# The next to last row stored as the last one is: x added on VectorE, plain stores by SyncE and ScalarE

## The chip, the cores and the metric

The kernel runs on 1 core of one Trainium2 chip. The metric is the time of one execution on the device, in microseconds (us). A profiled execution has a span, from its first to its last instruction, which is a little shorter than the time.

## The reference

```python
def reference(A_x, A_w_r, A_w_i, B_x, B_w1, B_b1, B_w2, B_b2):
    ...
    def _A_ref(x, w_r, w_i):                  # spectral filter over tokens and channels
        X = jnp.fft.rfft2(x) * (w_r + 1j * w_i)
        return jnp.fft.irfft2(X, s=(S, D))
    def _B_ref(x, w1, b1, w2, b2):            # MLP over the token axis
        h = _layernorm(x, axis=-1)
        u = _gelu(jnp.einsum("bsd,sf->bdf", h, w1) + b1)
        y = jnp.einsum("bdf,fs->bds", u, w2) + b2
        return y.transpose(0, 2, 1)
    x = A_x                                   # (1, 2048, 512) float32
    xn = _layernorm(x, axis=-1)
    s = _A_ref(xn, A_w_r, A_w_i)
    g = _silu(_B_ref(xn, B_w1, B_b1, B_w2, B_b2))
    return x + s * g
```

Tokens S = 2048, channels D = 512, hidden size F = 1792. Only the last operation, `x + s * g`, and how its result reaches the output are touched here.

## The kernel before

The 2048 tokens are laid out as 128 partitions by 16 rows (`NJ = 16`), so a row `j` is a tile of 128 tokens by 512 channels, 256 KB in float32. The kernel first normalizes and transforms the rows and forms the hidden layer (TensorE, with split high and low parts of the float32 operands), then filters the spectrum, and in its last part makes the outputs.

The last part is a loop over `p` from 0 to 7 (`NP = 8`). Pass `p` makes the gate `g` of two rows, `j0 = p` and `j1 = p + 8`, out of seven matrix products of half blocks taken in the order 1, 2, 5, 6, 3, 7, 4 (a Strassen scheme; `products`, `copied`, `summed`, `gate`). The weight blocks for it (`a11`, `a12`, `a21`, `s1`, `s4`) are loaded ahead from `w2`. The block `s1` of pass `p` lies in one of two tiles with the tag `s1`: in the pool `w2p` for even `p`, in the pool `fp` for odd `p`.

The spectral part `s` of a pair of rows is transformed back on TensorE into banks 0 and 1 of the accumulation memory (`spectral`), one pass behind the gates. `finish(g, j, cols)` then multiplies it by the gate on VectorE, in two instructions, because the channels are stored folded (`mirrored`), and stores the row in two halves of 64 partitions (`halved`).

Adding x is done in two ways. Early in the kernel, x is copied to the output for rows 0 to 14 (`out[q, :NJ - 1]`, L498), and `finish` for these rows adds `s * g` to it with an accumulating store issued by GpSimd (`accum_op`). For row 15 alone x is loaded into `xr` (SyncE, in the last pass at `k == 2`, into the tile `s1` of the pool `fp`, free once the pass's block `s1` is read), VectorE adds it, and the sum is stored plainly.

In passes 1 to 7 `finish` runs for the rows of the pass before. In the last pass it runs besides for that pass's own rows, 7 and 15: at `k == 5`, behind the sixth of the seven products, for row 7 whole and for row 15's right half (`right_`); after the loop, for row 15's left half, whose gate needs the seventh product. Those results go into the tile `rows` (`last_rows`). Stores of row 15 are issued by SyncE for partitions 0 to 63; for partitions 64 to 127 by SyncE for the right half and by ScalarE for the left.

In this last part each engine's instructions keep the order in which the program gives them. At the end of the program (shown in the profile as L1099) SyncE waits for all transfers to land, every engine runs a drain, and the engines meet.

Of the kernel before, what the change touches and what calls it, by code (L numbers as in the profile page):

```python
# [9 lines left out]
F32 = mybir.dt.float32  # L10
# [6 lines left out]
P = 128  # L17
S, D, F = 2048, 512, 1792
NJ = 16
NF = F // P  # L20
EPS = 1e-5
NH = NF // 2
# [120 lines left out]
def spectral_mixer_kernel(tc, x, w1, b1, w2, b2, wk, we, wx, c_f, c_ft, c_d, c_i, c_g, c_h, c_t, out):  # L143
    nc = tc.nc
    V, A, G, T, SY = nc.vector, nc.scalar, nc.gpsimd, nc.tensor, nc.sync

    def pool(stack, side, name, bufs):
        return stack.enter_context(tc.tile_pool(name=name, bufs=bufs, side=side, reuse_waits="tile"))


    def mirrored(t, turned):
        v = t.rearrange("p (h q c) -> p h q c", q=2, c=P)
        return v[:, :, 0], v[:, :, 1, ::-1] if turned else v[:, :, 1]
# [9 lines left out]
    with tc.tile_pool(name="ps", bufs=1, space=PSUM) as psp, ExitStack() as left, ExitStack() as right:  # L163
# [320 lines left out]
        for j in range(NJ):  # L484
# [49 lines left out]
            if more:  # L534
                low(w[1][1], raws[j + 1, 1], w[1][0])
                if FIRST <= j < FIRST + NE:
                    i = j - FIRST
# [210 lines left out]
        for n in range(8):  # L748
            a, b, c, d, e, f = PACE[n]
# [11 lines left out]
        w2p = pool(right, "right", "w2", 3)  # L761
        NP, HD = NJ // 2, D // 2
# [38 lines left out]
        def sums_of_blocks():  # L801
            added_up("a12", "s1")
            added_up("a11", "a12")
# [60 lines left out]
        def banks(p):  # L864
            return ps[:, 2 + p % 2, :HD], ps[:, 4, :HD], ps[:, 5, :HD]

        def products(p, n):

            wf = ready.pop(0)
            bx, by, bz = banks(p)  # L870
            o = {1: bx, 6: bx, 7: bx, 4: bx, 2: by, 5: bz, 3: bz}[n]

            for a, (wi, ui) in enumerate(((0, 0), (0, 1), (1, 0))):
                for m, i in enumerate(FORMS):
                    T.matmul(o, wf[:, wi, i], form_parts(n, i)[ui], start=m + a == 0 and n in (1, 2, 5),
                             stop=m == NH - 1 and a == 2, skip_group_check=n in (6, 3, 7, 4))

        def copied(name, src, where):
            t = where.tile([P, HD], F32, name=name, tag=name.split("_")[0], bufs=1)
            step(A.activation(t, src, AF.Copy))  # L880
            return t
# [16 lines left out]
        V, A, SY, G = (Kept(e, keep) for e in (nc.vector, nc.scalar, nc.sync, nc.gpsimd))  # L898
        fp = pool(left, "left", "fin", 1)
        halved = (slice(0, 64), slice(0, None, 2)), (slice(64, P), slice(1, None, 2))  # L900
# [5 lines left out]
        def new_gates(p):  # L906
            return [fp.tile([P, D], F32, name=f"g{j}", tag="g", bufs=4) for j in (p, p + NP)]
# [6 lines left out]
        def gathered(p):  # L914


            yt = fp.tile([P, 2, 4, 2, 64], F32, name=f"yt{p}", tag="yt")
            yts[p] = yt
            for i, j in enumerate((p, p + NP)):
                for h in range(2):  # L920
                    to = yt[:, i, :, h ^ i].rearrange("p b (s c) -> p b s c", c=2)
                    yield V.tensor_copy(to, ey[:, :, h::2, j]) if i else A.activation(to, ey[:, :, h::2, j], AF.Copy)
# [29 lines left out]
        def unfolded(p):  # L952

            es, y = new_sums(p) if p else first_sums
            e0, e1 = (es[:, :, k].rearrange("p i b c -> p i (b c)") for k in range(2))
            if "E" in PARTS[p]:
                first, odd = ps[:, 6, :256].rearrange("p (i s c) -> p i s c", s=2, c=64), ps[:, 6:8, 256:]
                other = y.rearrange("p i h q c -> p (i h q c)")[:, :257]
                A.activation(other, ps[:, 7, :257], AF.Copy)
                other = other[:, :256].rearrange("p (i s c) -> p i s c", s=2, c=64)  # L960

                V.tensor_add(es[:, :, 1, :, :64], first, other)
                V.tensor_sub(es[:, :, 1, 0, :63:-1], first[:, :, 0], other[:, :, 0])
                V.tensor_sub(es[:, :, 1, 1, :63:-1], other[:, :, 1], first[:, :, 1])
                V.tensor_add(e0, e1, odd)
                V.tensor_sub(e1, e1, odd)
            else:
                pe = ps[:, 6:8].rearrange("p i (h k) -> p i h k", h=2)
                A.activation(e1, pe[:, :, 1], AF.Copy)
                V.tensor_add(e0, pe[:, :, 0], e1)  # L970
                V.tensor_sub(e1, pe[:, :, 0], e1)
            yield
            u, v = es[:, :, :, 0], es[:, :, :, 1]
            V.tensor_add(y[:, :, :, 0], u, v)
            yield
            V.tensor_sub(y[:, :, ::-1, 1], u, v)
            ys[p] = y.rearrange("p i h q c -> p i (h q c)")
            yield
# [9 lines left out]
        def gate(g, j, cols, src, scale):  # L988
            A.activation(g[:, cols], src, AF.Silu, bias=b2t[:, j:j + 1], scale=scale)

        def summed(name, a, b):
            t = fp.tile([P, HD], F32, name=name, tag="c", bufs=2)
            V.tensor_add(t, a, b)
            return t

        def finish(g, j, cols):
            r = last_rows[:, j // NP] if last_rows is not None else fp.tile([P, D], F32, name=f"r{j}", tag="r", bufs=2)
            for to, a, b in zip(mirrored(r[:, cols], True), mirrored(ps[:, j // NP, cols], False), mirrored(g[:, cols], False)):
                V.tensor_mul(to, a, b)
            if j + 1 == NJ:  # L1000
                V.tensor_add(r[:, cols], r[:, cols], xr[:, cols])
            for queue, (rows, tokens) in zip((SY, SY if cols is right_ else A), halved):
                if j + 1 < NJ:
                    G.dma_start(out[tokens, j, cols], r[rows, cols], accum_op=ALU.add)
                else:
                    queue.dma_start(out[tokens, j, cols], r[rows, cols])

        yts, ys, pieces = {}, {}, iter(())
        last_rows = None

        for p in range(NP):
            j0, j1 = p, p + NP
            more = p + 1 < NP
            if p:
                gates[p] = new_gates(p)
            g0, g1 = gates[p]
            bx, by, bz = banks(p)
            slot, plan = SLOTS[min(p, 1) + (not more)]
            gathering = gathered(p)
            for k, n in enumerate(ORDER):  # L1020
                started = not p and k < 2
                if not started:
                    products(p, n)
                if n == 1 and p:
                    p1 = copied(f"p1_{p}", bx, w2p)
                elif n == 5:
                    p5 = copied(f"p5_{p}", bz, fp)
                elif n == 6:
                    v2 = copied(f"v2_{p}", bx, fp)
                elif n == 7:  # L1030
                    c22 = summed(f"c22_{p}", bx, p5)
                if not started:
                    ready.extend(w for w in [next(wforms, None)] if w is not None)
                if n == 2:
                    c11 = summed(f"c11_{p}", by, p1)
                elif n == 6:
                    gate(g0, j0, left_, c11, 1.0)
                elif n == 3:
                    gate(g0, j0, right_, summed(f"c12_{p}", bz, v2), 1.0)
                elif n == 7:  # L1040
                    gate(g1, j1, right_, c22, -1.0)
                elif n == 4:
                    gate(g1, j1, left_, bx, -1.0)
                if k == slot:
                    for part in PARTS[p]:
                        {"S": spectral, "E": even_channels, "O": odd_channels, "F": channels}[part](p - (part == "S"))
                    yts.pop(p)
                    pieces = unfolded(p)
                    if p:
                        for g, j in zip(gates.pop(p - 1), (j0 - 1, j1 - 1)):  # L1050
                            finish(g, j, whole)
                for what in plan.get(k, ""):
                    next(gathering if what == "g" else pieces)
                if more and n == 7:
                    sums_of_blocks()
                if not more and k == 2:
                    xr = fp.tile([P, NH * P], F32, name="xr", tag="s1", bufs=1)[:, :D]
                    for rows, tokens in halved:
                        SY.dma_start(xr[rows], x[tokens, NJ - 1])
                if not more and k == 5:  # L1060
                    spectral(p)
                    last_rows = fp.tile([P, 2, D], F32, name="rows", tag="yt")
                    finish(g0, j0, whole)
                    finish(g1, j1, right_)
# [38 lines left out]
```

## Time and profile before

| | us |
|---|---|
| time, median of 3 runs | 372.07 (371.99 to 372.15) |
| profiled execution, span | 370.2 |
| profiled execution, time beside its span | none given |
| TensorE busy (share of the span) | 360.1 (97%) |
| VectorE busy | 304.9 (82%) |
| ScalarE busy | 210.9 (57%) |
| GpSimd busy | 86.8 (23%) |
| last matrix product ends | 362.2 |
| last computation ends (VectorE, row 15's left half) | 363.7 |

The profiler calls TensorE's products PE and its weight loads PEld, VectorE DVE, ScalarE ACT, GpSimd POOL and SyncE SP; a q behind the name is the engine's queue of instructions (waits, drains, issues of transfers), which is not counted as busy. Nearly all instructions stand under L140, the helper `Kept`, which records every operation, so they are told apart by their tiles: `rows`, `r`, `xr`, `out_dram`. A row of a group or a timeline gives the output tile, an arrow and the input tiles, then shapes and count.

### The profile page before, as it was taken

To read this page: it belongs to the slowest core of one execution; us is meant where nothing else is said; L and a number is where in the kernel's file an instruction comes from. 1 tells how busy PE (TensorE), PEld (TensorE's weight loads), DVE (VectorE), ACT (ScalarE), POOL (GpSimd) and SP (SyncE) were. 2 spreads that over 40 slices of the span, in tenths; PEclk is the share of its full clock that TensorE was granted. 3 is DMA by queue.
4 is the path that set the end of the run, shared out by engine and by line. 5 is a ranking of instruction groups with operands and counts; after the bars stand their busy time and mean duration, and the time that the engine had idled before them with its cause. 6 is when DMAs were issued, how large, how long until landed. Compare 5 with 4: busy or idle time off the path is not lost.

```text
span 370.2 us, 8760 instructions
## 1 busy us (share of the span) xinstructions
PE 360.1 (97%) x3442; PEld 308.5 (83%) x3442; DVE 304.9 (82%) x585; ACT 210.9 (57%) x381; POOL 86.8 (23%) x128
## 2 busy tenths in 40 slices
PE   7999999999999999999999999999999999999991
PEld 4778888778777778777888999999898989898981
DVE  4799999974899988989994978696878788787971
ACT  3797887748634445655336686545564646464520
POOL 3133333332222012221020001040505050413131
PEclk9999999999999999999999999999999999999997
DMA  7976997505694698695585487797989899897443
GB/s 192 248 189 169 241 289 225 227 2 150 177 276 166 188 272 229 179 241 184 173 278 106 113 248 139 229 138 215 178 206 190 194 202 184 211 188 161 74 58 57
DMA packets 33289, 68.40 MB, mean 185 GB/s; under 512 B 4736, under 2 KB 19504, under 8 KB 33120
## 3 DMA queue, kind: packets, MB, share of 16 engines
q1 hardware_dynamic: 24192, 42.04, 41.1%
q0 software_dynamic: 8656, 25.27, 32.3%
q10 hardware_dynamic: 400, 0.52, 0.5%
q8 instruction: 27, 0.44, 0.5%
q14 instruction: 14, 0.11, 0.1%
HBM read 59.43 MB, written 8.13 MB: 183 GB/s over the span
## 4 chain that ended last, share of the span: by engine, by line
PE 94%; DMA 2%; DVE 1%; issue 0%; POOL 0%; ACT 0%; POOLq 0%
PE ps L140 94%; DMA x<-in_x_dram 2%; DVE stm L220 0%; DVE rows L140 0%; POOL w1r L431 0%; ACT g L140 0%; DVE w1l L448 0%; DVE mvm L230 0%; POOL qm L436 0%; DVE v2m L225 0%; DVE v2m L224 0%; POOLq L436 0%
## 5 line engine op out<-in xcount | busy, mean ns | idle before, releaser
L140 PE MATMUL ps<-h,w1h 128*128 128x512 f32 x400 | 116.5, 398 | 0.7 <-DVE nbm L239 0.7
L140 PEld LDWEIGHTS ps<-h,w1h 128*128 128x128 f32 x400 | 72.8, 188 | 20.6 <-issue 4.9
L140 PE MATMUL ps<-h,w1l 128*128 128x512 f32 x200 | 68.1, 392 | 0.3 <-DVE w1l L448 0.2
L140 DVE TENSOR_TENSOR w2f<-a,w2f 128x896 fp32r<-128x896 f32 x36 | 39.3, 1091 | 22.1 <-ACT w2f L140 22.1
L140 PEld LDWEIGHTS ps<-h,w1l 128*128 128x128 f32 x200 | 37.2, 188 | 9.8 <-DVE w1l L448 1.9
L140 ACT ACTIVATE w2f<-a 128x896 fp32r<-128x896 f32 x36 | 36.9, 1024 | 12.6 <-PE ps L140 8.0
L140 PE MATMUL ps<-fb,w2f 128*128 128x256 f32 x336 | 41.9, 279 | 0.0
L140 POOL DMA_DIRECT2D s<-in_w_dram x14 | 18.2, 1300 | 98.9 <-DMA s<-in_w_dram 49.9
L140 PE MATMUL ps<-fa,w2f 128*128 128x256 f32 x336 | 41.3, 278 | 0.0
L140 PEld LDWEIGHTS ps<-fb,w2f 128*128 128x128 f32 x336 | 39.7, 188 | 1.7 <-ACT g L140 0.8
L140 PE MATMUL ps<-fc,w2f 128*128 128x256 f32 x336 | 39.9, 277 | 0.0
L140 PEld LDWEIGHTS ps<-fa,w2f 128*128 128x128 f32 x336 | 39.8, 188 | 0.0
L140 PEld LDWEIGHTS ps<-fc,w2f 128*128 128x128 f32 x336 | 39.2, 188 | 0.0
L140 POOL DMA_DIRECT2D out_dram<-r x28 | 23.7, 1287 | 27.0 <-DVE r L140 27.0
L156 ACT ACTIVATE w1h<-w1s 128x512 fp32r<-128x512 f32 x26 | 16.2, 630 | 19.9 <-PE ps L140 16.4
L630 POOL DMA_DIRECT2D xc<-xc x16 | 9.8, 618 | 70.4 <-ACT xc L628 55.1
L286 POOL TENSOR_TENSOR ey<-t 128x256 f32<-128x256 f32 x16 | 15.7, 981 | 43.6 <-DVE t L284 43.6
L140 ACT ACTIVATE w2f<-s 128x896 fp32r<-128x896 f32 x15 | 15.3, 1021 | 13.6 <-PE ps L140 12.5
L448 DVE TENSOR_TENSOR w1l<-w1r,w1h 128x384 fp32r<-128x384 f32 x32 | 21.4, 667 | 0.3 <-ACT w1h L445 0.2
L140 PE MATMUL ps<-fd,w2f 128*128 128x256 f32 x168 | 20.6, 277 | 0.0
L140 ACT ACTIVATE g<-c,b2t 128x256 f32<-128x256 f32 x24 | 12.1, 505 | 14.6 <-DVE c L140 14.6
L140 PEld LDWEIGHTS ps<-fd,w2f 128*128 128x128 f32 x168 | 20.0, 188 | 0.1
(119 smaller groups left out, 600.9 us busy)
## 6 DMA issues: line engine op xcount, KB each, us to landing
a<-in_w_dram SPq DMA_DIRECT2D x22, 448.0 KB, 4.1
wt<-in_wk_dram POOLq DMA_DIRECT2D x16, 512.0 KB, 5.9
s<-in_w_dram SPq DMA_DIRECT2D x16, 448.0 KB, 5.3
s<-in_w_dram POOLq DMA_DIRECT2D x16, 448.0 KB, 6.4
w1s<-in_w_dram SPq DMA_DIRECT2D x52, 128.0 KB, 5.3
w1r<-in_w_dram SPq DMA_DIRECT2D x28, 192.0 KB, 6.1
xc<-xc POOLq DMA_DIRECT2D x16, 256.0 KB, 3.0
out_dram<-in_x_dram SPq DMA_DIRECT2D x4, 960.0 KB, 7.8
```

The source lines that it names most:

```text
L140: return lambda *args, **kw: self.keep(operation(*args, **kw))
L156: return A.activation(hi, src, AF.Copy), V.tensor_sub(lo, src, hi.bitcast(F32))
L286: G.tensor_add(ey[:, 0::3, :, j], a, b)
L448: keep(V.tensor_sub(dst, src, hi.bitcast(F32)))
L630: keep(G.dma_start(*(v.rearrange("p s t c -> p s (t c)") for v in (there[c::2], here[1 - c::2, ::-1]))))
```

## The change

Row 7, the next to last row made, is treated as row 15 is. Its x is loaded by SyncE in the last pass, into the `s1` tile of the pool `w2p`; VectorE adds it, 128x512 in one instruction; and its two halves are stored plainly, partitions 0 to 63 by SyncE and 64 to 127 by ScalarE. GpSimd's two accumulating stores of the last pass's rows are gone, so that GpSimd's last stores are those of rows 6 and 14. The early copy of x into the output still covers row 7, which is then overwritten.

```diff
             for to, a, b in zip(mirrored(r[:, cols], True), mirrored(ps[:, j // NP, cols], False), mirrored(g[:, cols], False)):
                 V.tensor_mul(to, a, b)
-            if j + 1 == NJ:
-                V.tensor_add(r[:, cols], r[:, cols], xr[:, cols])
+            if last_rows is not None:
+                V.tensor_add(r[:, cols], r[:, cols], xr[j // NP][:, cols])
             for queue, (rows, tokens) in zip((SY, SY if cols is right_ else A), halved):
-                if j + 1 < NJ:
+                if last_rows is None:
                     G.dma_start(out[tokens, j, cols], r[rows, cols], accum_op=ALU.add)
                 else:
                     queue.dma_start(out[tokens, j, cols], r[rows, cols])
...
                 if not more and k == 2:
-                    xr = fp.tile([P, NH * P], F32, name="xr", tag="s1", bufs=1)[:, :D]
-                    for rows, tokens in halved:
-                        SY.dma_start(xr[rows], x[tokens, NJ - 1])
+                    xr = [where.tile([P, NH * P], F32, name=f"xr{i}", tag="s1", bufs=1)[:, :D] for i, where in enumerate((w2p, fp))]
+                    for to, j in zip(xr, (j0, j1)):
+                        for rows, tokens in halved:
+                            SY.dma_start(to[rows], x[tokens, j])
```

## The prediction

> **What bounds the kernel now.** I read the page's chain first, because it names the engine whose work sets the end; then the chain in order of time for the last 50 us; then engine by engine the timeline of the last 12 us; and last the closing line of the kernel (L1099), since the chain stops well short of the span.
>
> The page's head, its engine row and its chain, and the last pieces of the chain in order of time:
>
> ```profile
> span 370.2 us, 8760 instructions
> PE 360.1 (97%) x3442; PEld 308.5 (83%) x3442; DVE 304.9 (82%) x585; ACT 210.9 (57%) x381; POOL 86.8 (23%) x128
> PE 94%; DMA 2%; DVE 1%; issue 0%; POOL 0%; ACT 0%; POOLq 0%
> ...
> 319.91 42.29 PE ps L140 x393
> ...
> 362.23 0.48 ACT g L140
> ...
> 362.73 0.50 DVE rows L140 x2
> ...
> 363.26 0.43 DVE rows L140
> ```
>
> The reader sees TensorE without a hole down to 362.2 us, then one activation, two multiplications and one addition: the last compute ends at 363.7. The span is 370.2. So 6.5 us at the end hold no computation, and the change lies wholly in that neighbourhood. Who uses those 6.5 us? The timelines of VectorE, ScalarE, SyncE and GpSimd around it:
>
> ```profile
> 359.75 1.15 DVE L140 TENSOR_TENSOR rows<-ps,g 128x256 f32<-128x256 f32 x4 [0.69 <-PE ps L140]
> 360.93 0.42 DVE L140 TENSOR_TENSOR rows<-rows,xr 128x256 f32<-128x256 f32 x1
> 362.73 0.49 DVE L140 TENSOR_TENSOR rows<-ps,g 128x128 f32<-128x128 f32 x2 [1.38 <-ACT g L140]
> ...
> 362.23 0.47 ACT L140 ACTIVATE g<-ps,b2t 128x256 f32<-128x256 f32 x1 [2.63 <-PE ps L140]
> 363.71 0.52 ACTq L140 DMA_DIRECT2D out_dram<-rows  x1
> ...
> 345.83 1.15 SPq L140 DMA_DIRECT2D xr<-in_x_dram  x2
> 361.39 2.79 SPq L140 DMA_DIRECT2D out_dram<-rows  x3
> ...
> 354.25 3.38 POOL L140 DMA_DIRECT2D out_dram<-r  x4 [10.79 <-DVE r L140]
> 360.80 1.67 POOL L140 DMA_DIRECT2D out_dram<-rows  x2 [3.17 <-DVE rows L140]
> ```
>
> The last plain stores go out at 363.71 on SyncE and ScalarE. GpSimd issues two stores of row 7 (the next to last row of this pair) from 360.80 to 362.47. Now the closing line: GpSimd's and SyncE's entries up to 366.45 (SyncE's last three once more by themselves), and GpSimd's after 369.41 (columns: count, min/median/max ns, first and last start):
>
> ```profile
> L1099 POOLq DRAIN  x1: 8202/8202/8202, 361.2 to 361.2; - x1
> ...
> L1099 SPq EVENT_SEMAPHORE  x9: 28/28/1032, 364.2 to 366.3; - x9
> L1099 SPq DRAIN  x2: 7/7/7, 366.4 to 366.4; - x2
> ...
> L1099 SPq EVENT_SEMAPHORE  x3: 28/28/28, 366.2 to 366.3; - x3
> ...
> L1099 POOLq EVENT_SEMAPHORE  x4: 17/17/17, 369.4 to 370.1; - x4
> L1099 POOLq DRAIN  x2: 46/70/93, 369.6 to 369.9; - x2
> ```
>
> This is the finding on which the rest stands. SyncE waits in its nine entries for every store's landing: the long one is 1.03 us, the last three start from 366.2 on, so the last landing comes at about 366.2, and SyncE is through at 366.4. GpSimd's drain, begun right behind its two stores, runs 8.2 us, from 361.2 to 369.4; only then comes GpSimd's meeting with the other engines, and 0.8 us later the span ends (369.4 to 370.2). From 366.4 to 369.4, 3.0 us, the core waits for that drain alone. The chain of the page cannot say so, because it follows busy instructions, and a drain is not counted as one. GpSimd's two later drains, with no store before them, took 93 and 46 ns.
>
> **The change part by part.** *Removed: two accumulating stores on GpSimd (row 7), and with them the place of its long drain.* GpSimd's last issues become the four of the previous pair (354.25 to 357.63). Where will the drain end then? Two anchors can be read, with the landings of GpSimd's last stores before and of the three last of the pair before it:
>
> ```profile
> L140 POOL DMA_DIRECT2D out_dram<-rows x2: 823/980/1137, 360.8 to 361.3; - x2
> DMA to landing us min/median/max: 3.1/3.6/4.1
> ...
> L140 POOL DMA_DIRECT2D out_dram<-r x3: 1137/1432/1747, 354.8 to 355.9; - x3
> DMA to landing us min/median/max: 4.4/4.4/4.8
> ```
>
> By the end of the issue: 369.4 - 362.47 = 6.9 us behind it, so 357.63 + 6.9 = 364.6. By the landing: the later store starts at 361.3 and lands 4.1 us on, at 365.4, so the drain outlasts it by 4.0; in the pair before, the last lands near 355.9 + 4.8 = 360.7, which gives 364.7. Both lie 1.8 us ahead of SyncE's 366.4, so I take the drain as off the end. What is late next is SyncE's wait for the last landings. The gain is 369.4 - 366.4 = 3.0 us, not the 4.8 by which the drain itself moves.
>
> The Trainium skill, in "VectorE: DVE Perf Modes", section "The DRAIN you can't avoid", says that the drains of preamble and postamble are a constant of about 12 ns on all five engines. By that rule GpSimd would hold nothing up, and the sum would be about 0 in place of -3.0 us. The row of 8202 ns disagrees, beside 7 ns on SyncE, so I go by the row.
>
> *Added on VectorE: one addition of 128x512 for row 7.* Not in the trace at this size for these tiles; the nearest rows, both operands and the result in on-chip memory as here, and the half-size addition itself:
>
> ```profile
> L140 DVE TENSOR_TENSOR y<-es x2: 681/682/684, 356.6 to 357.2; 128x512 f32<-128x512 f32 x2
> L140 DVE TENSOR_TENSOR rows<-rows,xr x2: 425/426/426, 360.9 to 363.3; 128x256 f32<-128x256 f32 x2
> ```
>
> Bounds: 0.43 below, 2 x 0.43 = 0.85 above; I take 0.68. Two of the four multiplications before 360.9 belong to row 7 and end near 360.5; the addition then runs to 361.2, and row 15's right half ends at 361.36 + 0.72 = 362.1 instead of 361.4. VectorE's next work starts at 362.73, released by ScalarE, which waits for TensorE's last product (362.20). 0.65 us stay free, so the cost is 0; at 0.85 it would be 0 too. If that cover were gone, the full 0.7 us would fall on the last chain.
>
> *Added on SyncE: one store (row 7, partitions 0 to 63).* SyncE's three stores now:
>
> ```profile
> L140 SPq DMA_DIRECT2D out_dram<-rows x3: 466/502/598, 361.4 to 363.7; - x3
> ```
>
> The new one waits for the new addition, to 361.25, and takes some 0.5 us. Then row 15's right half in two issues from 362.1 to about 363.25, and the left half's at 363.71 as before. Margin 0.45 us, cost 0. *Added on ScalarE: one store (partitions 64 to 127)*, 0.52 us by its own row, from 361.25 to 361.77. Queued behind it on ScalarE is the last activation, which cannot start before 362.23: margin 0.46, cost 0. If the addition came 0.5 us later than I say, this issue would push the activation and all that follows by the excess.
>
> *The landings of the last stores.* Now row 7 moves 256 KB by accumulation on GpSimd's queue, and row 15 another 256 KB as four stores of 64 KB. Afterwards the same 512 KB move by plain stores. The traffic before, in the stretches around the stores (columns: length, five engines, granted clock, DMA share, GB/s):
>
> ```profile
> 362.00:364.00 2.00, 0.19 (x2) 0.00 (x0) 0.91 (x3) 0.47 (x1) 0.47 (x1) 1.00 0.91 118
> 364.00:366.00 2.00, 0.00 (x0) 0.00 (x0) 0.00 (x0) 0.00 (x0) 0.00 (x0) 0.77 0.60 145
> ```
>
> The last stores are issued at 363.71 and SyncE is past the last landing at about 366.2: 2.5 us. Both the issue and this lag stay, so I take 0. At best, with the accumulating packets gone, the last stores land when those did, 365.4: 0.8 us sooner. At worst they find row 15's right half still ahead of them on the same queues, 128 KB or 0.9 us at 145 GB/s. Row 7's own 256 KB should be out of the way: issued at 361.3, with 2.5 us of lag and 2.2 us of traffic at 118 GB/s they are through at 366.0, ahead of the last landing. Bounds -0.8 and +0.9.
>
> *Moved ahead on SyncE: the loads of x.* Two loads become four. Row 15's pair waits, as now, for VectorE's last read of `s1` of the last pair (345.8). Row 7's pair takes the other `s1`, whose last reader was long through; SyncE issues it behind its load at 334.07:
>
> ```profile
> L140 DVE TENSOR_TENSOR w2f<-s,w2f x1: 1087/1087/1087, 325.5 to 325.5; 128x896 fp32r<-128x896 f32 x1
> 334.07 0.33 SPq L140 DMA_DIRECT2D a<-in_w_dram  x1
> 334.00:338.00 4.00, 4.00 (x63) 3.06 (x62) 1.80 (x4) 2.46 (x4) 0.86 (x1) 1.00 0.61 188
> 348.76 1.01 ACT L140 ACTIVATE w2f<-s 128x896 fp32r<-128x896 f32 x1
> 351.14 1.02 ACT L140 ACTIVATE w2f<-a 128x896 fp32r<-128x896 f32 x1
> L140 POOL DMA_DIRECT2D s<-in_w_dram x1: 858/858/858, 336.9 to 336.9; - x1
> DMA to landing us min/median/max: 5.2/5.2/5.2
> ```
>
> 256 KB more at 188 GB/s is 1.4 us of traffic between 335 and 338. The loads it can delay are `s4` (landing at 336.9 + 5.2 = 342.1, read at 348.76) and `a21` (issued at 334.07, read at 351.14): 6.7 us of cover and more, so 0. Without the cover 1.4 us would fall on TensorE.
>
> **Sum.** Against the profiled execution: 370.2 - 3.0 + 0 + 0 = 367.2 us of span. The page gives this execution no time beside its span; the three timed runs have a median of 372.07, 1.9 us above it. The part outside the span holds none of the changed work, so the forecast is 372.07 - 3.0 = 369.1 us, with -0.8 to +0.9 from the landings: 368.3 to 370.0.
>
> **The rivals.** *A: the drain waits for the whole core's stores, not for GpSimd's.* It ended 3.2 us after SyncE passed the last landing (366.2 to 369.4); if that lag is what it is, it stays at the end, and the time is 372.07 less at most the 0.8 of the landings, likeliest 372.0: no change. For it: GpSimd's last landing (365.4) and the core's (366.2) lie 0.8 us apart, and one long drain cannot tell which it followed. Against it: the drain began at 361.2, behind GpSimd's own issues. Chance 0.07.
>
> *D: the drain is not what the core waits for.* The view of waits for SyncE's queue over the last 8 us names TensorE, and TensorE's drain stands on the closing line:
>
> ```profile
> SPq L1099 <- PEq L1099: 3.6, 2, 3.2
> L1099 PEldq DRAIN  x1: 2227/2227/2227, 360.0 to 360.0; - x1
> ```
>
> If TensorE's sequencer, or anything else that the change leaves alone, held the meeting back, the 3.0 us would stay: 372.1, no change. Against it: that drain ended at 362.2, so it had long been done by 366.4, and GpSimd's entry follows its own drain at once. Chance 0.03. This is also where the rule of short drains in the Trainium skill, "VectorE: DVE Perf Modes", section "The DRAIN you can't avoid", would lead.
>
> *B, the other side: the drain pays per store issued just before it.* Two stores, 6.9 us behind the last issue, is 3.5 each; the previous pair has four issued in a row, so 13.9 us behind 357.63, 371.5, and the drain ends 2.1 us later than now: 374.2. It decides against the change from 2.95 us a store on (369.4 - 357.6, over four), and eats into the gain from 2.2 on (366.4 - 357.6, over four). For it: the four issues of that pair grow from 0.82 to 1.75 us as they queue. Against it: 0.85 us each is all that this growth shows. Chance 0.04.
>
> *C: the new stores delay the last landings.* If all of row 7's 256 KB still stands ahead of them, 1.8 us at 145 GB/s, SyncE is through at 368.2 and the time is 370.9. For it: the slice from 362 to 364 is 0.91 full. Against it: the accumulating packets that filled it are gone. Chance 0.05.
>
> **How the numbers follow.** Forecast 0.81, A 0.07, D 0.03, B 0.04, C 0.05. About 0.2%, 0.74 us, is what a measurement of this kernel can tell from no change. Faster by more than that: forecast and C, 0.86; within it: A and D, 0.10; slower: B, 0.04. The range 368.3 to 370.2 is the forecast's own with a little of the way to C, and leaves out A, B, D and most of C.
>
> **What would show it.** GpSimd's first drain on the closing line starts near 355.7 and ends near 364.6; SyncE's entries there again end near 366.4; the meeting follows at once, and the span ends 0.8 us behind them, near 367.2. VectorE shows a 128x512 addition of `rows` of about 0.68 us, and the last activation still starts at 362.2. A start of that activation after 362.3 would mean that ScalarE's new issue is in its way; a drain that still ends 3 us after SyncE's last wait would be A; one that lasts past 366.4 for itself, B. TensorE's end moving from 362.2 would mean that the earlier load costs something, and would make the prediction wrong in a place where I saw none.

## The result and the profile after

| | before | after |
|---|---|---|
| time, median of 4 runs, us | 372.03 (371.93 to 372.15) | 368.89 (368.51 to 369.14) |
| span of the profiled execution, us | 370.2 | 367.4 |
| time of that execution, us | none given | 369.14 |

The ratio is 0.9918, with a 95% interval of 0.9905 to 0.9932: the change takes 3.1 us off, 2.5 to 3.5.

The page after, its first lines:

```profile
span 367.4 us, 8767 instructions
PE 359.8 (98%) x3442; PEld 308.3 (84%) x3442; DVE 305.2 (83%) x586; ACT 210.5 (57%) x381; POOL 85.0 (23%) x126
```

The chain in order of time from 320 us on:

```profile
319.96 42.41 PE ps L140 x394
362.37 0.02 issue
362.40 0.48 ACT g L140
362.88 0.02 issue
362.90 0.50 DVE rows L140 x2
363.40 0.02 issue
363.43 0.42 DVE rows L140
```

The chain is that of before, 0.17 us later; that shift is there at 330 us already (SyncE's load of `a` starts at 329.98 in place of 329.80), ahead of anything that was changed, and TensorE's end lies between 361.7 and 362.7 in the traces of this study. So the ends are best compared from TensorE's end: 8.0 us before (362.2 to 370.2), 5.0 after (362.4 to 367.4). The whole gain is behind the last product.

The closing line, L1100 now: GpSimd's drains over the whole run, and SyncE's waits and its drains behind them:

```profile
L1100 POOLq DRAIN  x3: 46/93/8822, 355.7 to 367.1; - x3
...
L1100 SPq EVENT_SEMAPHORE  x9: 28/28/28, 364.4 to 366.5; - x9
L1100 SPq DRAIN  x2: 7/7/7, 366.5 to 366.6; - x2
```

GpSimd's long drain starts at 355.7 and lasts 8.8 us, to 364.6. SyncE is through at 366.6 and is now last; the span ends 0.8 us behind it. The drain has not become shorter. It has moved under work that was there anyway.

VectorE's timeline around the end:

```profile
359.92 0.76 DVE L140 TENSOR_TENSOR rows<-ps,g 128x256 f32<-128x256 f32 x2 [0.69 <-PE ps L140]
360.70 0.69 DVE L140 TENSOR_TENSOR rows<-rows,xr 128x512 f32<-128x512 f32 x1
361.31 0.48 DVE L140 TENSOR_TENSOR rows<-ps,g 128x128 f32<-128x128 f32 x2
361.83 0.42 DVE L140 TENSOR_TENSOR rows<-rows,xr 128x256 f32<-128x256 f32 x1
362.90 0.49 DVE L140 TENSOR_TENSOR rows<-ps,g 128x128 f32<-128x128 f32 x2 [0.65 <-ACT g L140]
```

ScalarE's:

```profile
361.43 0.54 ACTq L140 DMA_DIRECT2D out_dram<-rows  x1
362.40 0.47 ACT L140 ACTIVATE g<-ps,b2t 128x256 f32<-128x256 f32 x1 [2.63 <-PE ps L140]
```

SyncE's from 334 us on:

```profile
334.65 12.44 SPq L140 DMA_DIRECT2D xr<-in_x_dram  x4
361.42 2.92 SPq L140 DMA_DIRECT2D out_dram<-rows  x4
```

And GpSimd's last stores:

```profile
354.42 3.38 POOL L140 DMA_DIRECT2D out_dram<-r  x4 [10.79 <-DVE r L140]
```

The new addition takes 0.69 us, VectorE still waits 0.65 us for ScalarE's last gate, and ScalarE's new issue is done 0.43 us before that gate starts.

### The profile page after: what moved, and what is told of

It is laid out like the page before. It is cut to its first block, busy times and chain, and to the rows that moved or that the text cites. A ratio compares the mean times of both kernels' runs of the same rounds, so it can differ in the third digit from the quotient of the medians.

```text
span 367.4 us, 8767 instructions
## 1 busy us (share of the span) xinstructions
PE 359.8 (98%) x3442; PEld 308.3 (84%) x3442; DVE 305.2 (83%) x586; ACT 210.5 (57%) x381; POOL 85.0 (23%) x126
## 4 chain that ended last, share of the span: by engine, by line
PE 92%; DMA 3%; DVE 2%; SPq 1%; issue 0%; ACTq 0%; ACT 0%; DVEq 0%
PE ps L140 92%; DMA x<-in_x_dram 2%; DMA w1r<-in_w_dram 1%; SPq L198 1%; DVE w1l L448 0%; DVE rows L140 0%; DVE stm L220 0%; DVE h L448 0%; ACTq L431 0%; DVE tm L235 0%; ACT g L140 0%; SPq L431 0%; DVE ey L287 0%; DVE t L284 0%; DVE t L283 0%
## 5 line engine op out<-in xcount | busy, mean ns | idle before, releaser
L140 PEld LDWEIGHTS ps<-h,w1l 128*128 128x128 f32 x200 | 37.2, 188 | 10.2 <-DVE w1l L448 2.3
```

The lines of the kernel that those rows point to most:

```text
L140: return lambda *args, **kw: self.keep(operation(*args, **kw))
```

## The experiments

The open question after the result was not whether GpSimd's drain had held the end, but what it waits for. The prediction had two anchors that gave the same number here, the end of GpSimd's last issue and the landing of its last transfer; and a drain tied to accumulating stores, to any late work, or to the two configuration instructions that GpSimd runs at 6.4 us (in the expectations: its library of operations) would have done as well.

**First four: what must GpSimd do late for the drain to come back?** All start from the changed kernel.

```diff
+ (small)  G.dma_start(late[:, :64], w2_half(0, 0)[:, :64])   # behind finish(g0, j0, whole); late: tag s1 of w2p
+ (big)    G.dma_start(late, w2_half(0, 0))
+ (copy)   G.tensor_copy(late, last_rows[:, 0, D - 1:])       # late: a tile of 128x1
- (plain)  for queue, ... in zip((SY, SY if cols is right_ else A), halved):
+          for queue, ... in zip((G, G) if cols is whole else (SY, SY if cols is right_ else A), halved):
```

Small load:

> The changed kernel plus one small load on GpSimd late in the run: 128x64 of a weight block (32 KB) into the tile of row 7's x, free once VectorE has added it (about 361.4 us). Nothing uses it. It is neither a store nor accumulating. Theory (GpSimd's drain follows GpSimd's own last transfer, whatever its kind): the long drain is back on the path. Anchored to the end of the issue (6.8 to 6.9 us behind it in both traces): issue done at 362.1, drain to 369.0, time about 371.7. Anchored to the landing (3.6 to 4.0 us behind it): landing near 364.5, drain to 368.3, time about 371.0. Rival (only accumulating stores make the drain long): 368.9, no change against the changed kernel.

Big load:

> As the small load, but the whole weight block, 128x896 (448 KB), at the same place: the same issue, a later landing. Theory, drain anchored to the end of the issue: 369.1, time about 371.8, the same as with the small load. Drain anchored to the landing: landing near 367, drain to 370.8, time about 373.5, some 2.5 us more than with the small load. Rival (only accumulating stores): GpSimd's drain stays short, but SyncE waits for the landing near 367 and the time is about 369.9.

Copy:

> The changed kernel plus one copy of 128x1 on GpSimd behind row 7's addition (about 361.4 us): work late on GpSimd, but no transfer. Theory (the drain waits out GpSimd's transfers): the drain still ends near 364.6 or soon behind the copy, and the time is 368.9. Rival (the first drain of GpSimd takes its 8 us from wherever it starts): it starts near 361.4, ends near 369.5, and the time is about 372.0.

Plain stores by GpSimd:

> Half of the change undone: row 7 gets x added by VectorE, but GpSimd issues its two stores, plainly, at 361.4 and 362.0. Theory (any transfer of GpSimd): issue done at 363.1; drain anchored to the issue ends at 370.0, time about 372.6; anchored to the landing (361.96 + 3.6 = 365.6) it ends at 369.4, time about 372.0. Rival (it is the accumulation): 368.9.

Measured against the kernel before, which on that chip had a median of 371.75: small load 0.999 (0.9979 to 1.0002), big load 1.0042 (1.0024 to 1.0061), copy 0.9965 (0.9951 to 0.998), plain stores 0.9997 (0.9982 to 1.0012). For each run GpSimd's last work (timeline), and then its drains on the closing line.

Small load:

```profile
361.49 0.60 POOL L140 DMA_DIRECT2D late<-in_w_dram  x1 [3.90 <-DVE rows L140]
```

```profile
L1102 POOLq DRAIN  x3: 46/93/7474, 361.5 to 369.4; - x3
```

Big load:

```profile
361.05 0.60 POOL L140 DMA_DIRECT2D late<-in_w_dram  x1 [3.91 <-DVE rows L140]
```

```profile
L1102 POOLq DRAIN  x3: 46/102/8859, 361.0 to 370.4; - x3
```

Copy:

```profile
360.94 0.18 POOL L140 COPY late<-rows 128x1 f32<-128x1 f32 x1 [3.66 <-DVE rows L140]
```

```profile
L1102 POOLq DRAIN  x3: 46/93/6991, 360.9 to 368.4; - x3
```

Plain stores:

```profile
361.36 1.11 POOL L140 DMA_DIRECT2D out_dram<-rows  x2 [3.89 <-DVE rows L140]
```

```profile
L1100 POOLq DRAIN  x3: 51/93/7601, 361.8 to 369.9; - x3
```

Start and longest duration give the ends: 368.9, 369.9, 367.9, 369.4. One small load of 32 KB that nobody reads undoes nearly the whole gain. Plain stores do it as accumulating ones did, so accumulation is not the cause. The copy is the surprise: no new transfer at all, and yet the drain ends 6.8 us behind it (361.12 to 367.91). My theory of that run, that the drain waits out transfers in flight, had it end near 364.6. Its rival had the whole 8 us begin anew and the time at 372.0; neither is right, and the time lies between, at 370.1. So the drain has work of its own, which begins only when the engine is through with what stands before it. (A landing, here and below, is the last count of that transfer's semaphore in the trace.) The landing with a fixed 4 us behind it falls with the small load (landing 364.30, end 4.64 behind it) and the plain stores (364.55, 4.86). The issue with a fixed 6.8 us falls with the big load, 8.2 us behind its issue at 361.65.

**Next four: the covered costs, and the configuration instructions.**

```diff
  (after_again: the changed kernel)
- (no addition) V.tensor_add(r[:, cols], r[:, cols], xr[j // NP][:, cols])     # for row 7, and its load of x
+ (drain)       if p == NP - 2: G.drain()               # behind the finish of the pass before, in the changed kernel
- (no library)  G.tensor_mul(...), G.tensor_add(...), G.tensor_sub(...)        # 7 places, in the kernel before
+               keep(V.tensor_mul(...)), ...
```

The changed kernel again:

> The changed kernel once more, beside the runs that it is compared with: 0.991 to 0.993 of the kernel before, span near 367.2.

No addition:

> The changed kernel without row 7's load of x and without its addition; it leaves x out of row 7. Theory (both are covered): the same time as the changed kernel within 0.3 us; last activation still starts with TensorE's end. Rival (the addition's 0.69 us or the 256 KB at 335 us cost something): faster than the changed kernel by up to 0.7 us for the addition or more for the load.

A drain in pass 6:

> The changed kernel plus one drain on GpSimd in pass 6, behind the four stores issued near 340 to 343.6, where GpSimd is idle until 354.4. Theory F (each drain of GpSimd that follows work costs some 6.8 us behind it): the added drain ends near 350.4, the last one still near 364.5. Theory L (only the first drain after GpSimd has been given its library of operations, near 6 us in the trace, is long): the added drain is long, the last one under 0.2 us behind the last issue, near 357.9. The time is 368.9 either way.

No library:

> The kernel before, with GpSimd's multiplications, additions and subtractions (two-operand, early in the kernel) given to VectorE; GpSimd keeps its clearing, one copy and all transfers, and the two configuration instructions near 6 us go. Theory F: the last drain still ends 6.9 us behind the last issue, 3 us after SyncE's last wait; time 372.0 plus what VectorE's added work costs early. Theory L: the drain is short, the end is 0.8 us behind SyncE, and the time is 369.0 plus that cost. The early cost is unknown, between 0 and some 8 us (16 additions of 0.43 us and some small ones); the drain and the distance from TensorE's end to the span's end tell the theories apart whatever it is.

Measured: the changed kernel 0.992 (0.9903 to 0.9937); no addition 0.9907 (0.9892 to 0.9922), which overlaps with it, so in time the two cannot be told apart; in both traces the last gate starts 0.04 us behind TensorE's end, so neither the addition nor the loads stand in the path. Without GpSimd's two-operand operations the two configuration instructions are gone from the trace, the ratio is 1.0008 (0.9999 to 1.0018) and the drain is what it was, so they are not its cause. Its closing line:

```profile
L1099 POOLq DRAIN  x3: 46/93/8202, 361.7 to 370.4; - x3
```

The drain in pass 6 fits neither theory of its run; the added drain's row, and the closing line's:

```profile
L140 POOLq DRAIN  x1: 8486/8486/8486, 341.1 to 341.1; - x1
```

```profile
L1102 POOLq DRAIN  x3: 46/102/5267, 355.3 to 366.6; - x3
```

The added drain ends at 349.6, 6.4 us behind the last issue before it. The last one is neither as long as that nor gone: it ends at 360.5, 3.2 us behind its issue and 0.2 behind the last landing (360.33). A drain that comes soon after another has less left to do.

**What counts.** Take the number N of transfers that GpSimd has issued since its drain before (a short one at 0.3 us in the program, or the added one): 84 in the kernel before, 82 in the changed one. Against N the drains fall on one line: where no landing is late, they end 6.44 us behind the last work for N = 78, 6.77 to 6.79 for 82, 6.85 for 83, 6.93 for 84. That is 0.082 us a transfer. The big load and the last drain of the run above then fit if the work comes in two equal halves, and the second starts only when the last transfer has landed:

end = max(end of GpSimd's last work + 0.041 N, last landing) + 0.041 N + 0.04 us.

The halves are a fit; no trace shows them apart. This was put together from the runs above. The last four were to test it on drains that it had not seen.

```diff
+ (early drain, old stores) if p == NP - 2: G.drain()      # in the kernel before
+ (many)                    for i in range(6 * more): G.dma_start(<tile of 128x64>, w2[0, :, :64])   # head of passes 0 to 6
+ (drain in pass 2)         if p == 2: G.drain()           # in the changed kernel
+ (traffic)                 the copy above, and SY.dma_start(<tag s1 of w2p>, w2_half(0, 0))
```

Early drain with the old stores:

> The kernel before, with GpSimd storing and accumulating row 7 as it did, plus one drain on GpSimd in pass 6 behind the four stores near 343.5, where GpSimd is idle until 354. Nothing else is changed. Theory N (a drain of GpSimd works off the transfers issued since its last drain, 0.082 us each in the traces so far, half of it only after the last of them has landed): 6 transfers remain for the last drain, it ends 0.25 us behind their landing (365.4), near 365.7, SyncE is last at 366.4, and the time is that of the changed kernel, 369.0. Rival (a fixed 6.8 to 6.9 us behind GpSimd's last work): 372.0.

Many small loads:

> The changed kernel plus 42 small loads on GpSimd, 32 KB each, six at the head of each of the passes 0 to 6, into tiles that nobody reads; GpSimd's last issue stays near 357.8. Theory N: 124 transfers at 0.082 us, the last drain ends 10.1 us behind the last issue, near 367.9, behind SyncE, and the time is about 370.4. Rivals (a fixed 6.8 us; or by bytes, where 1.3 MB on 25 MB add 0.35 us): the drain ends near 364.6 to 364.9 and the time is 368.9. Either way the time can be longer if the small loads hold back the weight blocks that GpSimd accumulates; TensorE's end would show that.

Drain in pass 2:

> The changed kernel plus one drain on GpSimd in pass 2, behind the stores near 264.8. 54 of GpSimd's 82 transfers lie before it, 28 behind. Theory N: the last drain waits for the landing (360.9), and ends 28 x 0.041 = 1.15 us behind it, near 362.1; the added one ends some 2.2 us behind its last landing. Rivals: fixed 6.8 us, 364.6; only the first drain long, 361.1.

Traffic:

> The changed kernel plus the copy of 128x1 on GpSimd behind row 7's addition, and at the same time a load of a weight block, 448 KB, issued by SyncE (with GpSimd issuing it, the drain took 8.2 us behind the last issue in place of 6.8). Theory N: GpSimd has no landing to wait for, the drain ends 6.8 us behind the copy as without the load. Rival (the drain's own accesses are slowed by the traffic): 8.2 us behind the copy.

Early drain with the old stores, the added drain, GpSimd's last stores and the closing line:

```profile
L140 POOLq DRAIN  x1: 8481/8481/8481, 341.2 to 341.2; - x1
```

```profile
360.62 1.68 POOL L140 DMA_DIRECT2D out_dram<-rows  x2 [3.17 <-DVE rows L140]
```

```profile
L1101 POOLq DRAIN  x3: 51/102/4628, 361.0 to 366.8; - x3
```

Drain in pass 2, the added one and the closing line:

```profile
L140 POOLq DRAIN  x1: 7677/7677/7677, 264.6 to 264.6; - x1
```

```profile
L1102 POOLq DRAIN  x3: 51/102/6097, 355.8 to 367.1; - x3
```

Traffic, GpSimd's copy and the closing line:

```profile
361.66 0.18 POOL L140 COPY late<-rows 128x1 f32<-128x1 f32 x1 [3.67 <-DVE rows L140]
```

```profile
L1103 POOLq DRAIN  x3: 46/102/6991, 361.6 to 369.1; - x3
```

Many small loads, the closing line:

```profile
L1102 POOLq DRAIN  x3: 51/93/10069, 355.3 to 366.6; - x3
```

| drain | N | last work | last landing | end by the formula | end |
|---|---|---|---|---|---|
| early drain, old stores: added | 78 | 343.29 | 346.16 | 349.72 | 349.73 |
| early drain, old stores: last | 6 | 362.30 | 365.37 | 365.65 | 365.65 |
| drain in pass 2: added | 54 | 266.62 | 269.99 | 272.25 | 272.25 |
| drain in pass 2: last | 28 | 357.82 | 360.69 | 361.88 | 361.87 |
| traffic | 82 | 361.85 | 360.78 | 368.61 | 368.63 |
| many small loads | 124 | 357.34 | 360.25 | 367.55 | 365.36 |

Five of six to 0.02 us, and the sixth missed by 2.2: with 42 small loads more, the drain became 1.25 us longer, not 3.4. It ended at 365.4, ahead of SyncE's 366.1, and the time stayed at 0.9928 (0.9902 to 0.9954), where I had expected 370.4 us. That the drain goes by the number of transfers holds between 4 and 84 here; what flattens it by 124 (a limit on what GpSimd keeps, or small loads that count less when many are queued) stays open. One small load by itself counted in full, 0.08 us.

Two rivals of the number are packets and bytes. GpSimd's queue on the pages (packets, MB, share) of the kernel before, the plain stores, the changed kernel, the small load and the many small loads:

```profile
q0 software_dynamic: 8656, 25.27, 32.3%
q0 software_dynamic: 8592, 25.27, 32.1%
q0 software_dynamic: 8496, 25.01, 32.4%
q0 software_dynamic: 8528, 25.04, 31.6%
q0 software_dynamic: 9840, 26.39, 33.2%
```

The first two differ by 64 packets and not in their drains (6.93 and 6.94 us); the small load adds 0.4% of packets and 0.1% of bytes, and 1.2% to the drain, which is one transfer in 82. So up to 84 the number fits and these two do not. For the many small loads, scaling the changed kernel's 6.7 us by packets would add 1.1 us, by bytes 0.4, by number 3.4; measured 1.25. Packets come nearest there, but they do not fit the other runs.

The early drain with the old stores is the strongest single test. It keeps GpSimd's two accumulating stores at the end, adds one instruction where GpSimd has 10 us of idle time, and measures 368.83 us, 0.9917 (0.9895 to 0.994): the gain of the change, without the change. The two do not add up, since with either SyncE's wait is last: the changed kernel with a drain in pass 6, or in pass 2, took 368.67 and 369.27 us in one run each. The one run with traffic took 371.2.

## Why the prediction was right

*What bounds the end.* Right, and for the reason given: the 3.0 us between SyncE's last wait and GpSimd's drain went, and nothing else. Measured 3.1 by time, and 3.0 from TensorE's end to the span's end.

*Where the drain goes.* Forecast to end at 364.6 to 364.7, it ended at 364.6. The figure was right, but each of its two anchors was only half of the rule: the drain has some 6.8 us of work behind the last issue here because 82 transfers lie behind it, and would have followed the landing had that been late. By the formula the landing counts here from 361.15 us on, and it came at 360.93. That both anchors gave the same end was luck, and the choice between them cost nothing in this case.

*What is late next.* SyncE, forecast at 366.4, was through at 366.6, and 0.17 of that is TensorE's later end. The term of the landings was taken as 0, between -0.8 and +0.9. The last landing itself came sooner, 2.2 us behind the issue in place of 2.5 (363.88 to 366.09, against 363.71 to 366.18). That was given back: SyncE passes its waits in a fixed order of nine, and the one for ScalarE's last store stands third now. SyncE's waits from 366.1 on:

```profile
L1100 SPq EVENT_SEMAPHORE  x7: 28/28/28, 366.1 to 366.5; - x7
```

Seven waits are passed from the last landing on; before, the prediction's row had three. They go at 0.06 us each.

*The covered costs.* The addition, taken as 0.68 us, took 0.69. The margins of ScalarE's issue and of VectorE, forecast at 0.46 and 0.65, were 0.43 and 0.65. Row 7's load of x went out at 334.65 as forecast. Whether it delays GpSimd's accumulation of `s4`, which I priced at 1.4 us, is not shown: `s4` landed 6.3 us behind its issue in place of 5.2, but the second trace of the changed kernel has 5.2 again. All ten traces with that load have 5.0 to 6.3, the four without it 5.0 to 5.2. A delay of up to 1.1 us, if there is one, is hidden. The row of that transfer, by its tile:

```profile
L140 POOL DMA_DIRECT2D s<-in_w_dram x1: 858/858/858, 337.1 to 337.1; - x1
DMA to landing us min/median/max: 6.3/6.3/6.3
```

*The rivals.* A, that the drain follows the whole core's stores, falls with the trace after: it ended 1.5 us before the core's last landing. B, a price for each store issued just before, falls in its size: four stores in a row led to 6.77 us, not 13.9. Its kind of mechanism was nearer to the truth than I gave it credit for; the price is per transfer, but 0.082 us, and over all of them since the last drain. C did not come. D falls with the gain: TensorE's drain was left alone, and the meeting came 2.8 us sooner. For GpSimd the rule of the Trainium skill, "VectorE: DVE Perf Modes", section "The DRAIN you can't avoid", that such drains take a constant of about 12 ns, does not hold here: its long drain on the closing line had from 4.6 to 10.1 us in these traces.

## What to carry to other kernels

Look at the queue's entries on the closing line when a span ends long after the last computation: an engine that does not stand at the chain's end can be the one that everybody meets last. If GpSimd issues many transfers, either let its last work end early enough (some 7 us before the others here), or put a drain into an idle stretch of GpSimd late in the kernel; both were worth the same 3 us. Once that is hidden, the next limit here is the last store's landing. GpSimd's drain then ends 2.0 us ahead of SyncE's waits (364.6 against 366.6), so I would expect nothing from moving more work off GpSimd; no run tried it.

## What the runs showed of the hardware that I had not expected

GpSimd's drain is not a fixed cost. In these runs it took 0.082 us for each transfer that GpSimd had issued since its drain before, from 4 to 84 transfers, by the fit half of it only after the last of them had landed, and it began only when the engine's earlier work was done: behind a copy of 0.18 us, with every transfer landed 0.8 us before, it still took 6.8 us. Neither the kind of the last work (accumulating store, plain store, load, copy), nor 448 KB of other traffic beside it, nor GpSimd's two configuration instructions changed it. Why 124 transfers took 8.0 us and not 10.2 is not known.
